# A spectral kernel on one core: halved last inverse step, joined matmul groups, fewer and larger transfers

## The chip, the cores and the metric

The kernel runs on one core of a Trainium2 chip. The core has five engines that work side by side: TensorE (PE, matmuls; its weight loads are listed as PEld), VectorE (DVE), ScalarE (ACT), GpSimd (POOL) and SyncE (SP, which here only issues transfers). Each executes its own instructions strictly in the order of the program and waits on semaphores for the others. Transfers run on 16 DMA engines that the core's queues share. The metric is the time of one execution on the chip in microseconds (us), before and after the change; lower is better.

## The reference

Two independent halves are computed from fp32 inputs and laid side by side in the output (2048 x 1024):

```python
# A: Fourier mixing, 2048 positions x 512 channels
a = jnp.einsum("bsd,ed->bse", x, dft_hid_re)
b = jnp.einsum("bsd,ed->bse", x, dft_hid_im)
y = jnp.einsum("ts,bse->bte", dft_seq_re, a) - jnp.einsum("ts,bse->bte", dft_seq_im, b)
# B: a long convolution of 512 channels over 2048 positions, 128 states per channel
P = jnp.exp((A * dt[:, None])[:, :, None] * pos[None, None, :])
K = 2.0 * jnp.einsum("dn,dnl->dl", C, P).real            # the taps
y = jnp.fft.irfft(jnp.fft.rfft(u_t, L2) * jnp.fft.rfft(K, L2)[None], L2)[:, :, :L]
return y + u * D_skip[None, None, :]
```

## The kernel before

**The stream (class `Fnet`).** Half A is a long run of 1920 matmuls of 128x128 weights on 512 columns, all from line L366. An operand tile is split into a high and a low part (`hi` by ACT at L221, `lo` by DVE at L225), and each product is three matmuls: hi by hi, hi by lo, lo by hi. The stream takes 160 tiles ("items") of 256 KB, 12 matmuls to a tile. Of 160 items 132 come through a buffer `raw` (L334, SP's queue; `RAWS` = 7 of them) and 28 through POOL's queue (`SOFTS`). `DEPTH` = 4 is the number of `hi`/`lo` pairs, so of split tiles waiting for PE. Sums are evacuated by ACT (L389) and stored.

**Half B (class `Ssm`).** DVE builds tables `t1` and `t2` of powers, chunk by chunk, 16 chunks of 32 channels (L605 multiplies, L614 adds, L628, L634). `taps` (L801) multiplies the two tables of a chunk on PE, 128 recorded matmuls on tiles of 128 rows and 32 columns of the array. `stage1_k` (L832) and `stage1_u` (L890) are the first step of the forward transforms of the taps and of the input `u`; they store to DRAM (`xk`, `xu`). The channels are then worked off in four quarters, h = 0 to 3, and each quarter in four parts, q = 0 to 3:

- `load_spectrum` (L965) loads `xt` from `xu` and from `xk`, two transfers of 256 KB each;
- `product` does the second step of the transform (L992, PE), copies to SBUF (L1006, ACT), multiplies the two spectra (L1009, L1011, L1019, L1022, DVE), and does the first inverse step (L1029, PE, on the constant `ia`); ACT copies the sum out (L1044) and `store_z` (L1053) stores `z` to DRAM `zs`, two transfers of 256 KB;
- when all four parts of a quarter are stored, `inverse` runs twice for it: it loads `zl` from `zs`, does the last step (L1078, PE: 16 fp32 matmuls of 128 rows on 64 columns of the array, 128 columns wide, recorded as 32), copies out (L1084) and stores to `out_yb`.

A matmul on plain fp32 operands is recorded twice and each record has its weight load, so L801's 64 matmuls of a chunk are 256 instructions on PE's queue.

**What sets the order.** All engines' programs are written out by one planner (class `Plan`) that runs when the kernel is built. Each piece of work is a generator that yields the engine and the duration it expects; the planner lets the piece that can start first go first, and among those equal to 0.05 us the one of lower urgency number. The stream has urgency 5, so groups of half B are put between its matmuls. `Event` and `Sem` stand for readiness and for buffers. The two double banks of PSUM for half B (`banks`, `give`) are such buffers: a `taps` takes one, a `product` and a first inverse step two each. `Joined` can let a waiting first inverse step ride with the next `taps`: it is then issued directly ahead of it on PE, in the same two banks. With `JOIN` = 0 no quarter does that. `LATE` is the urgency of a quarter's product. The buffers of quarters 0 to 2 (`sets[0]`) exist once; those of `sets[1]` exist twice and are made when the tables' memory is free, after the last taps.

Of the kernel before, what the change touches and what calls it, by code (L numbers as in the profile page):

```python
# [24 lines left out]
def fft_constants():  # L25
# [16 lines left out]
    i = np.zeros((32, 2, 2, 32))  # L42
    i[:, 0, 0], i[:, 0, 1], i[:, 1, 0], i[:, 1, 1] = np.cos(chi), np.sin(chi), -np.sin(chi), np.cos(chi)
    ia = np.tile(i.reshape(32, 2, 64), (4, 1, 1))
    om = 2 * np.pi * ((4 * s[:, None, None] + 1) * (l2[None, :, None] + 32 * l1[None, None, :]) % 8192) / 8192
    ib = np.stack([np.cos(om), -np.sin(om)], axis=1).reshape(128, 32, 64) / 1024
    return [np.ascontiguousarray(a.astype(np.float32)) for a in (f1u, f1k, w2, ia, ib)]
# [3 lines left out]
STREAM = 5  # L51
GRAIN = 0.05
# [3 lines left out]
LATE = 1, 1, 3, 1  # L56
# [26 lines left out]
class Plan:  # L83
# [12 lines left out]
    def step(self, p, value):  # L96
        self.now = p[0]
        while True:
# [15 lines left out]
            else:  # L114
                if r[0] != p[5]:
                    p[0] += HOP
                elif r[0] == "dve" and len(r) < 4:
                    p[0] += RESULT
# [76 lines left out]
class Fnet:  # L195
# [112 lines left out]
    def soft(self, i):  # L308
        return i[0] == "s" and (2 * i[1] + i[2], i[3]) in SOFTS

# [117 lines left out]
class Ssm:  # L428


    def __init__(self, tc, ctx, plan, fnet, nd, ldt, dsk, uG, f1u, f1k, w2, ia, ib, out):
        self.tc, self.nc, self.plan, self.fnet = tc, tc.nc, plan, fnet
        self.nd, self.ldt, self.uG, self.out = nd, ldt, uG, out
# [486 lines left out]
    def quarters(self):  # L920
# [10 lines left out]
        self.plan.spawn(self.products(), 1)  # L931
        for h in range(4):
            self.plan.spawn(self.inverses(h), 1)

    def take(self):
        yield self.xu_ev
        for h in range(3):
            for q in range(4):
                yield self.sets[0].xts
                xt = self.sets[0].pool.tile([128, 2, 4, 2, PART], F32, name="xt")  # L940
                self.xt[h, q] = [[xt[:, r]] for r in range(2)]
                self.plan.set(self.take_ev[h, q])
        for q in range(4):
            self.xt[3, q] = []
            for r in range(2):
                yield self.fnet.x_free[8 + 2 * q + r]
                self.xt[3, q].append(self.fnet.spare(8 + 2 * q + r, [128, 2, 2, PART]))
            self.plan.set(self.take_ev[3, q])

    def spectra(self, name, x, evs):  # L950
        yield self.const2_ev
        yield self.set_ev[0]
        for h in range(4):
            view = x[h].rearrange("(q x g) c l d -> q (g c l) x d", q=8, x=4)
# [26 lines left out]
    def product(self, b, h, q, got, done):  # L981
# [3 lines left out]
        for r in range(2):  # L985
            for c in range(2):
                for xx in range(4):
                    xt = self.xt[h, q][r]
                    xt = (xt[xx * len(xt) // 4])[:, xx % (4 // len(xt))]
# [34 lines left out]
        def run(got):  # L1024
            for c, Y in enumerate((u, t)):
                for g in range(2):
                    for xx in range(4):
                        rows = slice(32 * xx, 32 * xx + 32)
                        nc.tensor.matmul(got[xx // 2][1][64 * g:64 * g + 64, xx % 2, :2 * PART], self.ia[rows, c],  # L1029
# [29 lines left out]
    def inverses(self, h):  # L1059

        yield self.zs_ev[h]
        b = self.sets[h // 3]
# [30 lines left out]
ISSUE = 1.0  # L1093
# [74 lines left out]
```

## Time and profile before

| | |
|---|---|
| median of 3 runs | 582.6 us (582.21 to 583.75) |
| the profiled execution's own time | 582.56 us |
| its span, first to last instruction | 580.8 us |
| granted TensorE clock | 0.999 of full speed |
| PE busy / DVE / ACT / POOL | 571.1 / 512.5 / 371.2 / 40.3 us |
| instructions on PE | 6150 matmul records, 6150 weight loads |
| moved by DMA | 133.10 MB, 229 GB/s mean |

The profile is one execution. Its span is 1.76 us shorter than the time of that execution, which is 0.04 us under the median. Busy shares are means over stages with different limits: the tables fill DVE until about 488 us, and behind them DVE has little to do. A line such as "PE f L1029 x32" in the chain of waits is one group of 32 recorded matmuls; its time there runs from the group's first matmul to the first one of what follows, so it is what the group occupies on PE, while the duration of a single matmul (400 ns in the stream) overlaps with the next.

### The profile page before, as it was taken

To read this page: it belongs to the slowest core of one execution; us is meant where nothing else is said; L and a number is where in the kernel's file an instruction comes from. 1 tells how busy PE (TensorE), PEld (TensorE's weight loads), DVE (VectorE), ACT (ScalarE), POOL (GpSimd) and SP (SyncE) were. 2 spreads that over 40 slices of the span, in tenths; PEclk is the share of its full clock that TensorE was granted. 3 is DMA by queue.
4 is the path that set the end of the run, shared out by engine and by line. 5 is a ranking of instruction groups with operands and counts; after the bars stand their busy time and mean duration, and the time that the engine had idled before them with its cause. 6 is when DMAs were issued, how large, how long until landed. Compare 5 with 4: busy or idle time off the path is not lost.

```text
span 580.8 us, 15376 instructions
## 1 busy us (share of the span) xinstructions
PE 571.1 (98%) x6150; PEld 436.1 (75%) x6150; DVE 512.5 (88%) x911; ACT 371.2 (64%) x729; POOL 40.3 (7%) x60
## 2 busy tenths in 40 slices
PE   8999999999999999999999999999999999999996
PEld 6877777788777777778877777777687777776685
DVE  6999999999999999999999999999989999346410
ACT  4779665763777595768568585945588744445522
POOL 0000000000100000100000001001100000000000
PEclk9999999999999999999999999999999999999999
DMA  8999999986469767876797887479989995789564
GB/s 248 327 372 263 280 294 276 285 262 170 133 159 239 207 171 218 205 180 207 207 222 190 237 216 226 125 186 296 243 280 262 243 282 184 209 251 303 169 195 144
DMA packets 147831, 133.10 MB, mean 229 GB/s; under 512 B 47280, under 2 KB 107312, under 8 KB 147504
## 3 DMA queue, kind: packets, MB, share of 16 engines
q1 hardware_dynamic: 139408, 117.05, 66.7%
q0 software_dynamic: 8064, 14.68, 12.6%
q8 instruction: 48, 0.79, 0.6%
q10 hardware_dynamic: 288, 0.39, 0.2%
q14 instruction: 23, 0.19, 0.1%
HBM read 89.36 MB, written 42.73 MB: 227 GB/s over the span
## 4 chain that ended last, share of the span: by engine, by line
PE 70%; DVE 23%; issue 4%; DMA 2%; SPq 0%; ACT 0%; DVEq 0%; ACTq 0%
PE acc L366 55%; DVE prod L605 8%; DVE t L614 4%; PE f L992 4%; PE f L801 3%; DVE lo L225 3%; PE f L1029 3%; PE f L1078 2%; PE f L890 2%; DVE t L634 1%; PE f L832 1%; DVE z L1009 1%; DVE cs L675 1%; DMA zl<-zs 1%; DVE uk L1011 1%
## 5 line engine op out<-in xcount | busy, mean ns | idle before, releaser
L366 PE MATMUL acc<-hi,x_hi 128*128 128x512 f32 x640 | 258.2, 403 | 0.3 <-ACT hi L221 0.3
L366 PE MATMUL acc<-lo,x_hi 128*128 128x512 f32 x640 | 250.2, 391 | 0.0
L366 PE MATMUL acc<-hi,x_lo 128*128 128x512 f32 x640 | 249.7, 390 | 0.1
L605 DVE TENSOR_TENSOR prod<-t,cs 128x1024 f32<-128x1024 f32 (+4 forms) x192 | 163.1, 867 | 1.7 <-ACT t L723 0.6
L366 PEld LDWEIGHTS acc<-hi,x_hi 128*128 128x128 f32 x640 | 120.1, 188 | 49.8 <-issue 23.7
L366 PEld LDWEIGHTS acc<-hi,x_lo 128*128 128x128 f32 x640 | 120.3, 188 | 26.5 <-DVE x_lo L225 0.5
L366 PEld LDWEIGHTS acc<-lo,x_hi 128*128 128x128 f32 x640 | 120.3, 188 | 23.0 <-DVE lo L225 0.2
L221 ACT ACTIVATE hi<-raw 128x512 fp32r<-128x512 f32 x132 | 82.6, 627 | 64.0 <-PE acc L366 48.5
L225 DVE TENSOR_TENSOR lo<-raw,hi 128x512 fp32r<-128x512 f32 x132 | 90.1, 684 | 28.2 <-ACT hi L221 21.9
L614 DVE TENSOR_TENSOR t<-prod 128x512 f32<-128x512 f32 (+4 forms) x192 | 94.0, 511 | 1.0
L621 ACT ACTIVATE square<-t 128x256 f32<-128x256 f32 (+1 forms) x64 | 36.7, 573 | 31.0 <-DVE t L614 28.3
L320 POOL DMA_DIRECT2D lo<-in_sT x28 | 24.3, 868 | 214.1 <-ACT lo L318 33.8
L1006 ACT ACTIVATE uk<-f 128x1024 f32<-128x1024 f32 x32 | 31.1, 1017 | 11.8 <-PE f L992 11.8
L801 PEld LDWEIGHTS f<-t,t 128*32 128x32 f32 x2048 | 29.5, 110 | 7.9 <-issue 5.8
L801 PE MATMUL f<-t,t 128*32 128x64 f32 x2048 | 32.4, 220 | 1.9 <-issue 1.4
L389 ACT ACTIVATE y<-acc 128x512 f32<-128x512 f32 x47 | 28.0, 595 | 8.7 <-PE acc L366 8.6
L1009 DVE TENSOR_TENSOR z<-uk 128x512 f32<-128x512 f32 x32 | 21.9, 684 | 9.6 <-ACT uk L1006 7.4
L315 POOL DMA_DIRECT2D hi<-in_sT x28 | 16.2, 577 | 189.4 <-PE acc L366 147.0
L1044 ACT ACTIVATE z<-f 128x512 f32<-128x512 f32 x32 | 17.7, 592 | 13.3 <-PE f L1029 13.3
L634 DVE TENSOR_TENSOR t<-square 128x128 f32<-128x128 f32 (+1 forms) x64 | 24.6, 385 | 0.0
L992 PE MATMUL f<-xt,w 64*32 64x256 f32 x768 | 23.5, 379 | 0.0
L1011 DVE TENSOR_TENSOR uk<-uk 128x512 f32<-128x512 f32 x32 | 22.1, 690 | 0.9
(94 smaller groups left out, 490.7 us busy)
## 6 DMA issues: line engine op xcount, KB each, us to landing
raw<-in_sT SPq DMA_DIRECT2D x99, 256.0 KB, 5.4
p<-y SPq DMA_DIRECT2D x32, 256.0 KB, 3.2
xk<-xk_sb SPq DMA_DIRECT2D x32, 256.0 KB, 5.2
zs<-z SPq DMA_DIRECT2D x32, 256.0 KB, 3.3
zl<-zs SPq DMA_DIRECT2D x16, 512.0 KB, 5.0
raw<-p SPq DMA_DIRECT2D x32, 256.0 KB, 4.4
hi<-in_sT POOLq DMA_DIRECT2D x28, 256.0 KB, 4.6
lo<-in_sT POOLq DMA_DIRECT2D x28, 256.0 KB, 4.9
```

The costliest lines, as they stand in the source:

```text
L221: self.nc.scalar.activation(hi, src, AF.Copy)
L225: self.nc.vector.tensor_tensor(lo, src, hi.bitcast(F32), op=OP.subtract)
L366: nc.tensor.matmul(acc[d], l[:, cols], r, start=k == 0 and n == 0, stop=k == len(items) - 1 and n == 2)
L389: self.nc.scalar.activation(y, ps, AF.Copy, scale=-1.0 if g[2] == 1 else 1.0)
L605: self.nc.vector.tensor_tensor(p.rearrange("p k d c m -> p k (d c) m"), src.rearrange("p d c l -> p (d c) l")[:, None, :, rows].to_broadca ...
L614: self.nc.vector.tensor_tensor(dst[:, :, :, rows], p[:, 0], p[:, 1, :, ::-1], op=OP.add)
L621: self.nc.scalar.activation(sq, t[:, :, :, m // 2:m], AF.Square)
L634: self.nc.vector.tensor_tensor(t[:, :, 0, m:2 * m:2], box[0][:, :, 0], box[0][:, :, 1], op=OP.subtract)
L801: nc.tensor.matmul(ps[32 * j:32 * j + 32, i], t1[:, d, c], t2[:, d, c], start=c == 0, stop=c == 1, tile_position=(0, 32 * j))
L992: nc.tensor.matmul(got[r][1][32 * xx:32 * xx + 32, g, 256 * c:256 * c + 256], self.w2[rows, 2 * q + r, xx, 32 * c:32 * c + 32], xt[rows].r ...
L1006: a.activation(uk[:, r].rearrange("p g c n d -> p g (c n d)"), p, AF.Copy)
L1011: v.tensor_tensor(t[:, r], t[:, r], u[:, r, :, ::-1], op=OP.mult)
```

## The change

What it does, part by part:

1. **The last inverse step of quarters 2 and 3 is halved.** The 64 rows of z are taken as two halves: every second output position needs only their sum and the others only their difference. `inverse2` loads `zl` with the two halves side by side, DVE forms their sum (`zsum`) and difference (L1095, L1097 of the new kernel, four instructions of 128x512 to an inverse), and PE multiplies them with a new constant `ib2`, on tiles of 64 rows and 32 columns of the array: 32 fp32 matmuls of 128 columns, recorded as 64, in place of 16 recorded as 32. The constant `ia` gets a second half that carries the phase this needs. `ib2` (512 KB) is loaded when the tables' memory is free. Both quarters use the doubled buffers of `sets[1]`.
2. **The first inverse step of quarters 0 and 1 rides with taps** (`JOIN` from 0 to 2): eight groups of 32 records go directly ahead of eight `taps`.
3. **Spectra and z in half as many transfers:** 512 KB in one instead of 256 KB in two, for `xt` of quarters 0 to 2 and for all `zs`.
4. **Numbers of the planner:** `RAWS` from 7 to 5, `DEPTH` from 4 to 5, the urgency of quarter 2's product from 3 to 1. The set `SOFTS` holds the same 28 items as before. The planner writes the whole program anew.

Line numbers in what follows are the new kernel's where the row is marked as such: L366 becomes L370, L801 L805, L992 L998, L1029 L1035, L1053 L1058, L965 L970, L225 L229, L1022 L1028; the last step of quarters 0 and 1 is L1126 and that of 2 and 3 L1104.

In PE's order a joined group has no stream between its two halves. Before, the first group of the first inverse step in the program (its last rows here; `f` are the two double banks, `uk` the product) was followed by the stream (L366):

```order
L1029 MATMUL f_2429<-uk,ia 64x256 x2
L1029 MATMUL f_2430<-uk,ia 64x256 x2
L366 MATMUL acc<-hi,x_hi_322 128x512
L366 MATMUL acc<-lo,x_hi_322 128x512
L366 MATMUL acc<-hi,x_lo_323 128x512
```

After, the same group (now L1035) is followed at once by the 64 matmuls of a taps (L805, on the two tables `t`), and then the stream (L370):

```order
L1035 MATMUL f_2575<-uk,ia 64x256 x2
L1035 MATMUL f_2576<-uk,ia 64x256 x2
L805 MATMUL f_2575<-t_124,t_2083 32x64 x64
L370 MATMUL acc<-hi,x_hi_452 128x512
L370 MATMUL acc<-lo,x_hi_452 128x512
```

The first inverse step has moved to the front of a taps. Over the whole program the stretches of stream between such groups fall from 72 to 63.

At the end of PE's order, before, the very last step of the last quarter was 16 matmuls on `zl`:

```order
L366 MATMUL acc<-hi,x_lo_5734 128x512
L1078 MATMUL f_7331<-zl,ib 64x128 x16
L366 MATMUL acc<-hi,x_hi_5770 128x512
L366 MATMUL acc<-lo,x_hi_5770 128x512
L366 MATMUL acc<-hi,x_lo_5771 128x512
```

After, it is 32 matmuls of half the rows and half the columns of the array, in pairs that take the sum and the difference by turns (the last two pairs here):

```order
L1104 MATMUL f_7402<-zsum,ib_6661 32x128 x2
L1104 MATMUL f_7402<-zl,ib_6661 32x128 x2
L370 MATMUL acc<-hi,x_hi_5551 128x512
L370 MATMUL acc<-lo,x_hi_5551 128x512
L370 MATMUL acc<-hi,x_lo_5552 128x512
```

Behind the last such group stand 15 stream matmuls before and 9 after; between the last group of the first inverse step and the first last-step group behind it stand 66 before and 78 after.

On DVE the new rows (`zsum`, `zl`) stand in the last part of the program, the first eight between the products of quarter 3 (one stretch of it after the change):

```order
L1097 TENSOR_TENSOR zl<-zl 128x512
L1015 TENSOR_TENSOR z<-uk 128x512
L1017 TENSOR_TENSOR uk<-uk 128x4x128
L1095 TENSOR_TENSOR zsum<-zl 128x512
L1097 TENSOR_TENSOR zl<-zl 128x512
```

All sixteen stand behind the last row of the tables. Up to and with that row DVE's program has 855 instructions before and 854 after, and they differ by kind in one row: 136 splits of the stream (L225) before, 135 after.

The diff, cut to its core:

```diff
-LATE = 1, 1, 3, 1
+LATE = 1, 1, 1, 1
...
     def load_spectrum(self, name, h, q, view):
         yield "dma", load(512, 270), FAST
-        for r in range(2):
-            for p, xt in enumerate(self.xt[h, q][r]):
-                n = xt.shape[1]
-                self.nc.sync.dma_start(xt[:, :, "uk".index(name)], view[2 * q + r, :, n * p:n * p + n])
+        for p, xt in enumerate(self.xt[h, q]):
+            n = xt.shape[1]
+            self.nc.sync.dma_start(xt[:, :, "uk".index(name)], view[q, :, n * p:n * p + n])
         self.plan.set(self.xt_ev[name, h, q])
...
-                        nc.tensor.matmul(got[xx // 2][1][64 * g:64 * g + 64, xx % 2, :2 * PART], self.ia[rows, c],
+                        nc.tensor.matmul(got[xx // 2][1][64 * g:64 * g + 64, xx % 2, :2 * PART], self.ia[rows, q // 2 if h >= HALVED else 0, c],
                                          Y[rows, :, g, 0], start=c == 0, stop=c == 1, tile_position=(32 * xx, 64 * g))
...
     def store_z(self, h, q, t, sem):
-        view = self.zs[h].rearrange("(q x g) c l d -> q (g c l) x d", q=8, x=4)
+        view = self.zs[h].rearrange("(q x g) c l d -> q (g c l) x d", q=4, x=8)
         yield "dma", load(512, 270), FAST
-        for r in range(2):
-            self.nc.sync.dma_start(view[2 * q + r], t[:, r])
+        self.nc.sync.dma_start(view[q], t.rearrange("p r x d -> p (r x) d"))
...
         yield self.zs_ev[h]
-        b = self.sets[h // 3]
+        if h >= HALVED:
+            yield self.ib2_ev
+        b = self.sets[int(h >= min(HALVED, 3))]
         for i in range(2):
             yield b.zls
-            self.plan.spawn(self.inverse(b, h, i, 16), 1)
+            self.plan.spawn((self.inverse2 if h >= HALVED else self.inverse)(b, h, i, 16), 1)
+
+    def load_ib2(self):
+        yield self.set_ev[1]
+        yield self.zs_ev[1]
+        self.ib2 = self.sets[1].pool.tile([128, 16, 2, 32], F32, name="ib2")
+        yield "dma", load(512)
+        self.nc.sync.dma_start(self.ib2, self.ib2_in)
+        self.plan.set(self.ib2_ev)
+
+    def inverse2(self, b, h, i, n):
+
+        nc, c = self.nc, n // 2
+        z = b.pool.tile([128, 2, c, PART], F32, name="zl", bufs=b.n)
+        view = self.zs[h].rearrange("(a s) c l d -> (s c) a l d", a=2)
+        yield "dma", load(64 * n, 270), FAST
+        for y in range(2):
+            o = n * i + c * y
+            nc.sync.dma_start(z[64 * y:64 * y + 64], view[:, :, o:o + c])
+        t = b.pool.tile([128, c, PART], F32, name="zsum", bufs=b.n)
+        for w in range(0, c, 4):
+            m = slice(w, w + 4)
+            yield "dve", dve(512)
+            nc.vector.tensor_tensor(t[:, m], z[:, 0, m], z[:, 1, m], op=OP.add)
+            yield "dve", dve(512), *APART
+            nc.vector.tensor_tensor(z[:, 1, m], z[:, 0, m], z[:, 1, m], op=OP.subtract)
+        (k, ps), = yield from self.banks(1)
+        yield "pe", 1.06, None, 64
+        for o in range(0, c, 2):
+            for x in range(4):
+                for y in range(2):
+                    r, w = slice(64 * y, 64 * y + 64), o + x // 2
+                    nc.tensor.matmul(ps[32 * x:32 * x + 32, y, PART * (o // 2):PART * (o // 2) + PART],
+                                     self.ib2[r, c * i + w, x % 2], (t, z[:, 1])[x % 2][r, w], start=True, stop=True,
+                                     tile_position=(64 * y, 32 * x))
+        for y in range(2):
+            yield "act", act(512)
+            nc.scalar.activation(z[:, 0, 4 * y:4 * y + 4].rearrange("p w d -> p (w d)"), ps[:, y], AF.Copy)
+        self.give(k)
+        yield "dma", load(32 * n, 270)
+        nc.sync.dma_start(self.out[:, c * i:c * i + c, PART * h:PART * h + PART], z[:, 0])
+        self.plan.put(b.zls)
...
-CHUNK, FIRST, JOIN = 32, 128, 0
-RAWS, DEPTH, STAGED, AHEAD = 7, 4, 4, 3
+CHUNK, FIRST, JOIN = 32, 128, 2
+HALVED = 2
+RAWS, DEPTH, STAGED, AHEAD = 5, 5, 4, 3
```

More of the change, by code (lines that the diff above doesn't have):

```diff
@@ L939, in take @@
                 yield self.sets[0].xts
-                xt = self.sets[0].pool.tile([128, 2, 4, 2, PART], F32, name="xt")
-                self.xt[h, q] = [[xt[:, r]] for r in range(2)]
+                xt = self.sets[0].pool.tile([128, 8, 2, PART], F32, name="xt")
+                self.xt[h, q] = [xt]
                 self.plan.set(self.take_ev[h, q])
@@ L1126, in layout @@
     n = lambda a: np.asarray(a)
-    f1u, f1k, w2, ia, ib = fft_constants()
+    f1u, f1k, w2, ia, ib, ib2 = fft_constants()
     w = np.stack([n(A_dft_hid_re).T, n(A_dft_hid_im).T])
```

45 lines of the change are left out of this document (27 added, 18 removed).

## The prediction

> **What bounds the kernel now.** I read the page's busy times and slices first, then busy time by window, then the chain of waits, and at last single stretches of the timeline.
>
> ```profile
> span 580.8 us, 15376 instructions
> PE 571.1 (98%) x6150; PEld 436.1 (75%) x6150; DVE 512.5 (88%) x911; ACT 371.2 (64%) x729; POOL 40.3 (7%) x60
> ...
> DVE  6999999999999999999999999999989999346410
> ...
> 0.00:488.00 488.00, 483.20 (x5178) 370.22 (x5179) 476.46 (x855) 333.83 (x669) 40.27 (x60) 1.00 0.82 234
> 488.00:581.00 93.00, 87.92 (x974) 65.88 (x972) 36.00 (x57) 37.41 (x60) 0.00 (x0) 0.99 0.68 206
> ```
>
> The window rows give length, then PE, PEld, DVE, ACT, POOL, then the granted clock. Two engines are full until 488 us: PE idles 4.8 us of 488, DVE 11.5. Behind that DVE is busy 36.0 us of 93 and PE goes on alone at full clock. The border is the last row of the tables and the last taps:
>
> ```profile
> 487.48 0.68 DVE L614 TENSOR_TENSOR t<-prod 128x512 f32<-128x512 f32 x1
> ...
> 488.41 1.99 PE L801 MATMUL f<-t,t 128*32 128x64 f32 x128
> ```
>
> DVE ends its last table row at 488.16, a quarter of a microsecond before PE takes it up. So the time is the start of the last taps, which both engines set within that quarter, plus what PE still has to do, plus a tail. From the chain of waits (start, what the group occupies, count):
>
> ```profile
> 488.48 1.92 PE f L801 x128
> 490.40 2.26 PE acc L366 x9
> 492.67 1.05 PE f L1029 x32
> ...
> 497.03 11.79 PE acc L366 x51
> 508.82 1.90 PE f L1078 x32
> ...
> 516.38 1.89 PE f L992 x64
> ...
> 572.29 3.64 PE acc L366 x15
> ```
>
> A stream matmul costs (11.79 - 2.26) / (51 - 9) = 0.227 us, and a stretch of stream costs 2.26 - 9 x 0.227 = 0.22 us on top: the price of leaving and re-entering the stream. PE ends at 572.29 + 3.64 = 575.93, 87.45 us after the start of the last taps; the tail to the end of the span is 4.87 us.
>
> **The change part by part. Halved last step.** Four groups of 64 records take the place of four of 32 that occupy 1.90 us each. The nearest row is L992, the same tiles of 64 rows and 32 columns of the array: 64 records on 256 columns in 1.89. At 128 columns half its streaming remains: with 0.2 of entry and drain, 1.69 / 2 + 0.2 = 1.05 us. L1029, with half the records at the same 256 columns, agrees: 1.05. Gain 4 x 0.85 = 3.4 us. The bounds: nothing, if a record costs what it costs in L992 whatever its width; and 4 x (1.90 - 64 x 1.92 / 128) = 3.8 us at L801's pace of 15 ns to a record. I take 3.4, by L992's tile shape.
>
> [...]
>
> **Its DVE rows.** Sixteen rows of 128x512:
>
> ```profile
> L1009 DVE TENSOR_TENSOR z<-uk 128x512 f32<-128x512 f32 x32 | 21.9, 684 | 9.6 <-ACT uk L1006 7.4
> ```
>
> 16 x 0.684 = 10.9 us, all behind the last table row, where DVE idles 57 us. What they can delay is the last chain of quarter 3, from its z to the end:
>
> ```profile
> 551.80 1.09 ACT L1044 ACTIVATE z<-f 128x512 f32<-128x512 f32 x2 [2.18 <-PE f L1029]
> ...
> 556.20 1.76 SPq L1073 DMA_DIRECT2D zl<-zs  x4
> ...
> 566.85 1.97 PE L1078 MATMUL f<-zl,ib 128*64 128x128 f32 x32
> ...
> zs<-z SPq DMA_DIRECT2D x32, 256.0 KB, 3.3
> zl<-zs SPq DMA_DIRECT2D x16, 512.0 KB, 5.0
> ```
>
> After: copies 1.1, z's transfer at most 5.0 (512 KB, as `zl`), two issues 0.9 (four take 1.76), `zl` 5.0, four DVE rows 2.7: 14.7 us, against 78 stream matmuls, 17.9 us. Hidden with 3 us to spare; if the store's and load's landings grew by more than that, the excess would land on the end. The second half is wanted 3 us later and DVE gives it 2.7 later.
>
> **Joined groups and order.** Nine stretches of stream fewer, 9 x 0.22 = 2.0 us; one of them lies behind the last taps, eight ahead. The change of tiles between L1029 and L801 is never seen directly here, so the bounds are 0 and 9 x 0.3. More matters ahead of the taps: the first inverse step no longer starts as soon as its product is nearly ready. Before it did, and waited in the middle:
>
> ```profile
> 0.00:581.00 581.00, 20.24 (x512) 10.08 (x512) 1.00 0.80 229
> ...
> 547.29 1.12 PE L1029 MATMUL f<-uk,ia 32*64 32x256 f32 x32
> ...
> PE f L801 <- issue: 1.4, 1, 1.4
> PE f L832 <- DVE ks L824: 0.6, 1, 0.6
> ```
>
> The first row is PE's and PEld's busy time on line L1029 alone: 20.24 us for 16 groups, where an undisturbed one takes 1.12: 2.3 us of waiting on DVE. By the new order DVE has finished the product several rows ahead of each joined group, so I take the 2.3 us as gone, and the 0.6 at L832, whose rows also stand farther apart; bounds 0 and 2.9.
>
> **Instruction supply.** The 1.4 us of "issue" is one taps that ran dry:
>
> ```profile
> 405.56 1.88 PE L801 MATMUL f<-t,t 128*32 128x64 f32 x118
> 408.86 0.41 PE L801 MATMUL f<-t,t 128*32 128x64 f32 x10 [1.43 <-issue]
> ...
> q8 instruction: 48, 0.79, 0.6%
> ```
>
> 48 instruction transfers for 12300 instructions on PE is one to 256. A taps alone is 256 instructions in 1.92 us; joined it is 320 in 2.97, without the slow stream to catch up in. One of 16 taps ran dry before; of the eight long ones and the others I take three, 4.3 us in place of 1.4, two ahead of the last taps and one at it. Bounds: none, and all eight.
>
> [...]
>
> **Transfers, buffers, ranks.** Half the transfers for `xt` and `zs` move the same bytes; SP saves some 40 issues, and no group on PE waits long for a transfer, so I cost them at nothing. What covers a spectrum is the stream ahead of its product; if that cover went, one landing 1.7 us later (5.0 against 3.3) would be the price each time, for at most 12. `raw` falls by two and `hi`/`lo` rises by one pair, which brings splits nearer to PE's need earlier; nothing. `ib2` is 512 KB ahead of one `raw` on SP; nothing, at most one landing of 5.0 us, which five pairs in stock, 12 matmuls or 2.7 us each, cover. Quarter 2's earlier product doesn't delay the tables: 854 DVE rows stand up to the last table row, where 855 did.
>
> **The sum.** Start of the last taps: by PE, 488.48 + 12 more stream matmuls ahead of it (2.7) - 8 stretches (1.8) - 2.9 of waits on DVE - 1.4 of the old dry run + 2.9 of two new ones = 488.0. By DVE, one split fewer, 488.5 - 0.7 = 487.8. The later sets it: 488.0. Behind it: 87.45 - 12 stream matmuls (2.7) - 3.4 - one stretch (0.2) + one dry run (1.4) = 82.5. Tail 4.9: the last 512 KB of output leaves nearer to the end, but the last transfer is still the stream's. Span 575.4. The profiled execution took 582.56 for a span of 580.8, 1.76 more, and stands 0.04 under the median of 582.6: forecast 577.2 us, 0.9% faster.
>
> **Rivals.** (1) *The halved step isn't halved*: a record costs 29.5 ns as in L992 and the four groups stay at 1.89. For it: same tiles. Against: L801's 15 ns. Time 577.2 + 3.4 = 580.6, chance 0.04. A floor between the two paces, say 22 ns, leaves part: 64 x 0.022 + 0.2 = 1.6 us, 577.2 + 4 x 0.55 = 579.4, chance 0.03. [...]
>
> (2) *Banks.* A joined group holds both double banks until ACT has made three copies, and the next product needs both.
>
> ```profile
> L221 ACT ACTIVATE hi<-raw 128x512 fp32r<-128x512 f32 x132 | 82.6, 627 | 64.0 <-PE acc L366 48.5
> ```
>
> Three copies (two of L1044 take 1.09) are 1.6 us, two splits between them 1.25: 2.9, where the shortest stretch of stream behind a joined group is 12 matmuls, 2.7. With a hop on either side say 0.4 us for each of eight: 3.2, 580.4. Against: an item needs one split in 2.7 us, so mostly one stands between. Chance 0.09.
>
> (3) *Slower: instruction supply.* All eight joined groups run dry: five more than in the forecast, 577.2 + 5 x 1.43 = 584.4. With seven (582.9) the old time is back; the eighth makes it slower. For it: 320 instructions in a row exceed a transfer of 256. Against: the next transfer may already be there. Chance 0.08.
> (4) *The gain is eaten ahead of the taps* by waits that the planner didn't see, with the last taps 6 us later: 583. Chance 0.04.
>
> **Chances and range.** The forecast's case has 0.72; its own range is 573 (no dry run: DVE's 487.8 + 81.1 + 4.9 + 1.8 = 575.6, less 2.5 if DVE's 11.5 us of idle time shrink by a fifth) to 579.5. A difference of 0.3%, 1.75 us, is about what a measurement of this kernel can tell from none. Faster than that (under 580.85): the forecast, most of (1) and (2), 0.86; within it 0.06; slower 0.08. The range, 573.0 to 581.0, leaves out (3), (4) and the far ends of the others.
>
> **What would show it.** Right: groups of L1104 at 1.05 us, the last taps near 488, 82 us from there to PE's last matmul, PE's time on L1035 at 1.1 us to a group. Wrong: L1104 near 1.9; "issue" on L805 in more than four places; PE's waits on ACT copies ahead of L998; the last taps past 492.

## The result, and the profile after

The changed kernel takes 585.39 us (median of 9 runs, 583.77 to 589.58), the kernel before 582.40 on the same chip (9 runs, 581.67 to 584.42). The ratio is 1.0054, 95% interval 1.0036 to 1.0072: about half a per cent slower, where 577.2 us and 0.9% faster were forecast. The profiled execution of the changed kernel took 584.71 us, its span is 582.9.

The page of the changed kernel, busy times and two of its slices:

```profile
span 582.9 us, 15613 instructions
PE 567.2 (97%) x6278; PEld 434.4 (75%) x6278; DVE 524.8 (90%) x927; ACT 371.5 (64%) x729; POOL 40.5 (7%) x60
...
DVE  6999999999999999999999898999998999747723
...
PEclk9999999999999999999999899999999999999999
```

PE is busy for 3.9 us less than before, as the change meant, and yet the span is 2.1 us longer: PE waits more. New are the 8s in DVE's row, which was full up to the last table row, and one 8 in the granted clock, in the 23rd of the 40 slices (from 320.6 us). From the chain of waits of the changed kernel (start, us, what):

```profile
494.64 1.97 PE f L805 x128
...
537.76 9.12 DMA zs<-z
...
547.63 2.29 PE f L1104 x123
...
571.15 1.09 PE f L1104 x64
...
574.52 1.08 PE f L1104 x64
575.60 1.69 PE acc L370 x7
```

The last taps start at 494.6 us; before it was 488.5, forecast were 488.0. PE ends at 577.9 (the chain leaves the last two matmuls out), 83.3 us later; before 87.45, forecast 82.5. The halved groups take 1.09 us each against 1.90. So the stretch behind the last taps shrank nearly as forecast, and the start of the last taps slipped by 6.2 us. Where it slipped, PE's waits tell (the engine, the tile and line that waited, the releaser: us in total, times, longest):

```profile
PE f L1035 <- ACT zl L1132: 3.0, 1, 3.0
PE f L998 <- DMA raw<-in_wT: 1.8, 1, 1.8
...
PE f L1104 <- ACT z L1050: 1.3, 1, 1.3
PE acc L370 <- DMA lo<-in_sT: 1.2, 2, 0.8
PE acc L370 <- ACT y L393: 0.8, 1, 0.8
PE f L836 <- DVE ks L828: 0.4, 1, 0.4
PE f L805 <- issue: 0.4, 1, 0.4
```

The second row is the wait of a product (L998) at 416 us; its releaser is put down to another load of that moment, but what the product lacked was its spectrum, as the experiments show. The largest wait stands at 320 us. PE's timeline there (start, us, instructions, the wait before them and its releaser):

```profile
319.43 0.65 PE L1035 MATMUL f<-uk,ia 32*64 32x256 f32 x4
323.08 1.11 PE L1035 MATMUL f<-uk,ia 32*64 32x256 f32 x28 [3.00 <-ACT zl L1132]
324.12 3.57 PE L805 MATMUL f<-t,t 128*32 128x64 f32 x128
```

Busy time of the changed kernel by window, cut where the clock changes (length, PE, PEld, DVE, ACT, POOL, then the granted clock, third number from the right):

```profile
320.64:324.05 3.41, 0.97 (x28) 0.58 (x28) 3.41 (x6) 2.91 (x7) 1.28 (x2) 1.00 0.59 82
324.06:327.46 3.40, 3.40 (x134) 3.34 (x128) 3.37 (x5) 0.96 (x2) 0.00 (x0) 0.50 1.04 277
327.47:330.88 3.41, 3.41 (x38) 2.44 (x38) 1.84 (x4) 3.12 (x9) 0.00 (x0) 1.00 0.38 108
```

A joined group starts in the one free double bank, then waits 3.00 us for ACT to empty the other, in which the last step L1126 of quarter 0 lies. And the taps behind it take 3.57 us in place of 1.92, with no wait: the granted clock is 0.50 in that window and 1.00 on either side. So this place costs 3.6 us at the group, 3.0 of them the wait, and another 1.6 at the taps. The stretch at 0.50 lasts 3.41 us, and in the 3.41 us ahead of it PE is busy for 0.97.

ACT's rows of the same place show why the copy was late:

```profile
315.29 0.50 ACT L662 ACTIVATE seed<-seed 128x352 f32<-128x352 f32 x1 [2.94 <-DVE seed L660]
315.81 1.28 ACT L664 ACT_TABLE_LOAD   x1
317.10 0.50 ACT L664 ACTIVATE seed<-seed 128x352 f32<-128x352 f32 x1
317.62 1.28 ACT L666 ACT_TABLE_LOAD   x1
...
321.44 0.57 ACT L1132 ACTIVATE zl<-f 128x512 f32<-128x512 f32 x1
```

ACT waited 2.94 us for DVE's row L660 of a seed, then went through the seed's functions with two table loads (1.28 us each) and three rows of other work among them (0.6 us each), and only then came to the copy, whose bank PE had filled by 317.2.

### The profile page after: what moved, and what is told of

Its sections match the earlier page's. It is cut to its first block, busy times and chain, and to the rows that moved or that the text cites. A ratio compares the mean times of both kernels' runs of the same rounds, so it can differ in the third digit from the quotient of the medians.

```text
span 582.9 us, 15613 instructions
## 1 busy us (share of the span) xinstructions
PE 567.2 (97%) x6278; PEld 434.4 (75%) x6278; DVE 524.8 (90%) x927; ACT 371.5 (64%) x729; POOL 40.5 (7%) x60
## 4 chain that ended last, share of the span: by engine, by line
PE 57%; DVE 29%; issue 5%; DMA 4%; ACT 4%; DVEq 0%; ACTq 0%
PE acc L370 45%; DVE prod L609 10%; DVE t L618 6%; DVE lo L229 4%; PE f L998 3%; PE f L805 3%; PE f L1035 2%; PE f L894 2%; DMA zs<-z 2%; DVE t L638 1%; DVE z L1015 1%; DVE t L632 1%; PE f L1126 1%; DVE xk_sb L848 1%; DMA raw<-in_wT 1%
## 5 line engine op out<-in xcount | busy, mean ns | idle before, releaser
L370 PE MATMUL acc<-hi,x_hi 128*128 128x512 f32 x640 | 257.5, 402 | 0.9 <-ACT y L393 0.8
L370 PE MATMUL acc<-lo,x_hi 128*128 128x512 f32 x640 | 250.4, 391 | 1.2 <-DMA lo<-in_sT 1.2
L370 PE MATMUL acc<-hi,x_lo 128*128 128x512 f32 x640 | 249.9, 390 | 0.0
L609 DVE TENSOR_TENSOR prod<-t,cs 128x1024 f32<-128x1024 f32 (+3 forms) x192 | 163.5, 869 | 5.1 <-ACT t L747 3.1
L370 PEld LDWEIGHTS acc<-hi,x_hi 128*128 128x128 f32 x640 | 120.2, 188 | 47.9 <-issue 20.5
L370 PEld LDWEIGHTS acc<-hi,x_lo 128*128 128x128 f32 x640 | 120.3, 188 | 26.8 <-issue 0.4
L370 PEld LDWEIGHTS acc<-lo,x_hi 128*128 128x128 f32 x640 | 120.4, 188 | 25.2 <-DMA lo<-in_sT 2.1
L225 ACT ACTIVATE hi<-raw 128x512 fp32r<-128x512 f32 x132 | 81.6, 626 | 58.6 <-PE acc L370 45.1
L229 DVE TENSOR_TENSOR lo<-raw,hi 128x512 fp32r<-128x512 f32 x132 | 90.0, 684 | 23.2 <-ACT hi L225 18.6
L805 PEld LDWEIGHTS f<-t,t 128*32 128x32 f32 x2048 | 31.0, 114 | 6.7 <-issue 2.3
L805 PE MATMUL f<-t,t 128*32 128x64 f32 x2048 | 33.9, 226 | 0.4 <-issue 0.4
L998 PE MATMUL f<-xt,w 64*32 64x256 f32 x768 | 23.5, 379 | 1.8 <-DMA raw<-in_wT 1.8
L632 DVE SCALAR_TENSOR_TENSOR t<-t 128x128 f32<-128x128 f32 (+2 forms) x48 | 22.3, 466 | 0.5
```

Source lines behind the costliest of these rows:

```text
L225: self.nc.scalar.activation(hi, src, AF.Copy)
L229: self.nc.vector.tensor_tensor(lo, src, hi.bitcast(F32), op=OP.subtract)
L370: nc.tensor.matmul(acc[d], l[:, cols], r, start=k == 0 and n == 0, stop=k == len(items) - 1 and n == 2)
L609: self.nc.vector.tensor_tensor(p.rearrange("p k d c m -> p k (d c) m"), src.rearrange("p d c l -> p (d c) l")[:, None, :, rows].to_broadca ...
L632: self.nc.vector.scalar_tensor_tensor(t[:, :, 1, m:2 * m:2], t[:, :, 0, m // 2:m], 2.0, t[:, :, 1, m // 2:m], op0=OP.mult, op1=OP.mult)
L805: nc.tensor.matmul(ps[32 * j:32 * j + 32, i], t1[:, d, c], t2[:, d, c], start=c == 0, stop=c == 1, tile_position=(0, 32 * j))
```

## An account of PE's losses

To compare orders with each other, each kernel's PE time is taken apart in the same way: a stream matmul counts 0.2275 us, leaving and re-entering the stream 0.2, an undisturbed group 1.92 (taps), 1.05 (first inverse step), 1.90 (last step), 1.09 (halved) and 1.89 (product). What a group or stretch occupies beyond that is its loss (waits, "issue" and low clock alike). The groups of the first transform step (L836 and L894 of the new kernel) are left out; they lose 1.7 us before and 1.9 after. The kernel before loses 7.3 us in the profiled execution, the changed one 14.3. The work itself shrank by 4 x 0.81 = 3.2 us for the halved step and by about 2.0 for nine stretches. 580.8 - 5.2 + 7.0 = 582.6, and the tail is 0.2 longer: the span of 582.9 is accounted for. The losses of the changed kernel, place by place: 3.6 and 1.6 at the joined group and its taps at 319 to 328 us, 1.9 at the spectrum at 412, 1.4 at the first halved group at 545, 3.1 between 136 and 181 (before: 1.3 there), 0.6 at a taps at 354, and the rest under 0.6 each but for 1.2 at the start, which both have. Gone are the waits of the first inverse step on DVE (2.7) and the taps at 405 us with 1.43 us of "issue" in it (1.7).

| kernel | median us | ratio to before, 95% | last taps, us | PE's losses, us |
|---|---|---|---|---|
| before | 582.4 to 582.9 | 1 | 488.4 | 7.3 |
| changed | 585.4 | 1.0054 [1.0036, 1.0072] | 494.6 | 14.3 |
| e2 no halving | 587.9 | 1.0081 [1.0068, 1.0094] | 494.9 | 13.7 |
| e3 two transfers | 583.6 | 1.0016 [1.0002, 1.0030] | 493.9 | 12.0 |
| e4 halving alone | 581.0 | 0.9964 [0.9951, 0.9976] | 488.3 | 8.7 |
| e5 sines moved | 584.4 | 1.0020 [1.0001, 1.0040] | 492.6 | 12.7 |
| e6 joining alone | 600.7 | 1.0302 [1.0279, 1.0325] | 485.9 | 26.8 |
| e7 = e3 and e5 | 582.4 | 1.0013 [0.9985, 1.0041] | 491.9 | 12.1 |
| e8 halving, one transfer | 580.4 | 0.9959 [0.9945, 0.9972] | 488.3 | 8.1 |
| e9 = e7, t2's rows first | 581.7 | 0.9996 [0.9974, 1.0019] | 490.4 | 11.6 |
| e10 = e8, buffers 5 and 5 | 608.7 | 1.0442 [1.0421, 1.0462] | 482.2 | 31.1 |
| e11 = e8, planned anew | 585.9 | 1.0063 [1.0040, 1.0085] | 492.4 | 14.6 |
| e12 = e9, t1's row first | 581.7 | 0.9990 [0.9974, 1.0006] | 491.7 | 11.7 |
| e13 = e8, buffers for z | 580.9 | 0.9969 [0.9957, 0.9982] | 487.7 | 7.9 |

The median of before is that of the chip that ran the row's kernel. The ratio goes with the means of the runs, not with the medians: e7's runs average 583.4 us and before's on that chip 582.7. The last taps and losses are of one profiled execution each, and those of e3, e5 and e10 were 1.6, 1.3 and 5.7 us faster than their medians; in e6, e10 and e11 other work stands ahead of the last taps, so that only time and losses compare.

## The experiments

The theories at the start: A, the joined groups need both double banks, so ACT's copies in ACT's order, and this delays taps and tables; B, the larger transfers land later; C, any newly planned order comes out worse; D, the halved step's own rows and constant cost time.

**e2: no halving.** Quarters 2 and 3 use the plain last step.

```diff
-HALVED = 2
+HALVED = 4
```

> The changed kernel with the halved step off (HALVED = 4), so that quarters 2 and 3 use the plain last step again; joined groups, transfers and the planner's numbers as changed, and the order up to the last taps the same. Theory A (the joined groups, which need both double banks and so ACT's copies in order, delay the tables): the last taps stay at 494 to 495 us, and the time grows by the halving alone, 4 x (1.90 - 1.09) = 3.2 us, less the wait of 1.4 us at the first halved group if that goes with it: 586.5 to 588.6 us. Rival D (the halved step's own constant, buffers and DVE rows delay the tables): the last taps come back to 488 or 489 us and the time is 582 to 584 us.

587.88 us, as A had it. The last taps stay, at 494.86 us, and so do the waits for the banks and at the spectrum of 416 us (PE's waits in e2):

```profile
PE f L1035 <- ACT zl L1132: 2.7, 1, 2.7
PE f L998 <- DMA raw<-in_wT: 1.8, 1, 1.8
```

The halved step has no part in the slip (D falls), and it is worth 2.5 us of time in this order (587.88 - 585.39; the two ran on different chips, and by the ratios to before it is 1.6), 2.8 of span: the 3.2, less 0.6 that PE loses more with it.

**e3: two transfers** of 256 KB for each spectrum and each z, in the changed kernel's order.

```diff
-            self.nc.sync.dma_start(xt[:, :, "uk".index(name)], view[q, :, n * p:n * p + n])
+            for m in range(0, xt.shape[1], n):
+                o = xt.shape[1] * p + m
+                self.nc.sync.dma_start(xt[:, m:m + n, "uk".index(name)], view[q, :, o:o + n])
...
-        self.nc.sync.dma_start(view[q], t.rearrange("p r x d -> p (r x) d"))
+        for r in range(2):
+            self.nc.sync.dma_start(view[q, :, 4 * r:4 * r + 4], t[:, r])
```

> The changed kernel with two transfers of 256 KB again for each spectrum and each z; same plan on PE, DVE and ACT. Theory A: the last taps stay at 494 us within half a microsecond; of PE's wait of 1.9 us for a spectrum at L998 and of 1.4 us at L1104 a part goes, so the time is 583 to 585.5 us. Rival B (the larger transfers, which land later, delay the products and with them the tables): the last taps at 488 to 490 us, the time 577 to 581 us.

583.55 us, inside A's interval; B as the cause of the slip falls, since the last taps come at 493.9. Of the two waits on transfers one shrank and one went, and the joined group still waits (PE's waits in e3):

```profile
PE f L1037 <- ACT zl L1135: 3.2, 1, 3.2
...
PE f L1000 <- DMA xt<-xk: 0.7, 1, 0.7
```

**e4: halving alone**, with no joined groups, two transfers, and `RAWS`, `DEPTH` and `LATE` of before. PE's order up to the last taps is that of the kernel before.

```diff
-LATE = 1, 1, 1, 1
+LATE = 1, 1, 3, 1
...
-CHUNK, FIRST, JOIN = 32, 128, 2
+CHUNK, FIRST, JOIN = 32, 128, 0
...
-RAWS, DEPTH, STAGED, AHEAD = 5, 5, 4, 3
+RAWS, DEPTH, STAGED, AHEAD = 7, 4, 4, 3
```

> The halved step alone: no joined groups, two transfers, RAWS 7, DEPTH 4 and the urgencies of the kernel before. Theory A: the last taps are at 488.5 us within 0.7, and the stretch behind them is 87.45 less 4 x 0.81 = 84.2 us, so the time is 582.4 - 3.2 = 579.2 us, with 578.0 to 580.5 as bounds. Rival C (any newly planned order comes out some microseconds worse, whatever is changed): last taps past 491 us, time 582 to 585 us. Rival D (the halved step's rows and constant cost time): likewise 582 us and more, but with the loss behind the last taps.

580.96 us, a little over A's upper bound: 0.36% faster than before, not 0.55%. The last taps start at 488.34 as expected, so what is missing lies behind them. PE loses about 1 us at the first two halved groups, 0.6 of it in waits for ACT and DVE; their place in the chain of waits of e4 is this:

```profile
527.80 9.62 DMA zl<-zs
...
537.44 0.70 DVE zsum L1098
...
545.43 0.66 PE f L1107 x28
```

The load of `zl` ends 9.6 us after the step before it in the chain, and then eight rows of the halved step stand between DVE's other rows for 8 us. These rows were costed as hidden; at the last halved group they are, at the first one not quite. The tail is 0.9 us longer too.

**e5: three sine instructions moved.** In the changed kernel ACT's L666 (with its table load), L668 and L670 of one seed go behind the two copies L1132 for which the joined group waited; nothing else changes its place on any engine.

```diff
-        a.activation(r[:, 0:6], r[:, 0:6], AF.Sin, scale=-TWO_PI)
+        self.later(ck, lambda: a.activation(r[:, 0:6], r[:, 0:6], AF.Sin, scale=-TWO_PI))
...
-        self.give(k)
+        self.give(k), self.flush()
...
+    def later(self, ck, op):
+        if ck == 11:
+            self.held.append(op)
+        else:
+            op()
```

> The changed kernel with one thing moved: ACT's three sine instructions of one seed (L666 with its table load, L668, L670) stand behind the two copies L1132 for which the joined group at 319 us waited 3.0 us. Every other instruction keeps its place on its engine. Theory A: the joined group there waits 0.7 to 1.3 us instead of 3.0, DVE's gaps of 0.88 and 0.71 us behind it shrink, the last taps come at 492 to 493.2 us and the time is 583.0 to 584.0 us, 1.4 to 2.4 less than the changed kernel. Rival (the wait at 319 us is caught up or covered by another engine before the last taps, so it costs nothing): last taps at 494 to 495 us, the time as the changed kernel's within 0.6 us.

584.4 us, the last taps at 492.58: 2.0 us earlier, inside A's interval, though the median is 1.0 less than the changed kernel's rather than 1.4 to 2.4 (by the ratios to before on each one's chip, 2.0). The wait and the low clock are gone together. The joined group in e5's timeline:

```profile
320.99 1.11 PE L1035 MATMUL f<-uk,ia 32*64 32x256 f32 x28 [0.27 <-ACT zl L1132]
```

And e5's windows:

```profile
320.00:324.00 4.00, 3.37 (x133) 2.22 (x136) 3.93 (x8) 3.81 (x7) 0.86 (x1) 1.00 0.82 115
324.00:328.00 4.00, 4.00 (x80) 3.01 (x76) 3.96 (x6) 3.13 (x8) 0.00 (x0) 1.00 0.76 217
```

So at this place the low clock came with the wait. But of the 5.2 us that the place cost, only 2.0 reach the last taps; the group and its taps still lose 1.5, and 1.2 more are lost at the spectrum of 412 us, which the product now reaches earlier than its load lands (PE's waits in e5):

```profile
PE f L998 <- DMA raw<-in_wT: 3.0, 1, 3.0
```

**e7: both edits together.**

> The changed kernel with both single edits together: two transfers of 256 KB for each spectrum and each z, and ACT's three sine instructions behind the copies that the joined group at 319 us waits for. If the two waits are separate and add up: no clock below 0.95 ahead of 500 us, last taps at 491 to 492.3 us, the stretch behind them 81 to 82 us, time 579.5 to 582 us. If a wait that is taken away only moves to another place (a PE wait of over 2 us elsewhere): last taps past 493 us and 583 us or more.

582.35 us (the first reading had an upper bound of 582), the last taps at 491.85, no clock under 0.95 ahead of 500 us. On the last taps the two edits add up: 0.6 us in e3 alone, 2.0 in e5 alone, 2.7 of the 6.2 us together. But the second reading came true in part: PE's wait for the spectrum is 2.1 us, as the next experiment shows, longer than e3's 0.7, because the product now comes to it earlier. The stretch behind the last taps is 83.8 us, not 81 to 82, with 1.0 us of waiting at the first halved group again.

**e9 and e12: the rows of the next tables first.** DVE's largest gap in the joined order is 1.6 us at 358 us, ahead of the first rows of the next tables. e9 lets ACT write t2's first rows ahead of its copies for z and ks there, e12 the row of t1 too (the last line of the diff is e12's).

```diff
+            (h, q, n) == (1, 1, 0) and self.first_rows(11); a.activation(z[:, :, 2 * n:2 * n + 2].rearrange("p r x d -> p x r d"),
...
+    def first_rows(self, n):
+        a, cs, t = self.nc.scalar, self.cs[n], self.t2
+        a.activation(t[:, :, :, 1].rearrange("p d c -> p c d"), cs[:, :, 0, :, 0], AF.Copy)
...
+        self.early = self.tab.tile([128, CHUNK, 2, 32], F32, name="t1", bufs=2)
```

> The kernel with both single edits, and one more thing moved: at 356 us ACT writes the first rows of the next table t2 (L747, L750) ahead of the two copies of z (L1052), the copy of the taps (L815) and the seed's L684, not behind them; nothing else changes its place. Theory A (in the joined order ACT's copies for half B stand ahead of the rows for which DVE waits): DVE's gap of 1.62 us there goes or falls below 0.5, the last table row and the last taps come 1.0 to 1.6 us earlier, at 490.3 to 490.9 us, and the time falls by about as much, to 580.8 to 581.5 us. Rival (another engine sets the last taps, DVE's gap is spare time): last taps at 491.5 us or later, the time as with both edits alone (582.35) within 0.6 us.

> As the kernel before it in this series, but the one copy L727 (first row of the next t1, which DVE's second row there reads) goes ahead of the copies of z and of the taps as well. In that kernel DVE's gap at 357.7 us stayed at 1.76 us, now put down to L727. Theory A: the gap falls below 0.5 us and the last table row comes 1.0 to 1.6 us earlier than the 490.35 us there, if the load of a spectrum at 409 us lands alike (PE's wait there 0.7 us): last taps 488.9 to 489.5, time 580.2 to 580.9 us. Rival (the gap is spare time, and the 1.4 us by which the last taps came earlier there were the load's alone): last taps at 490 us or later, the time 581.65 within 0.6 us.

In e9 the last taps came at 490.42 us, as A had it, but not for A's reason: the gap stayed, and the time of 581.65 us lies between the two readings. In e12 it stayed too, and the last taps were back at 491.65, with 581.74 us, as the rival had it. DVE's row behind the gap, which waited 1.62 us for ACT's L747 in e7, in e9's timeline:

```profile
359.49 0.40 DVE L609 TENSOR_TENSOR prod<-t,cs 128x128 f32<-128x128 f32 x1 [1.76 <-ACT t L727]
```

And in e12's:

```profile
359.65 0.38 DVE L609 TENSOR_TENSOR prod<-t,cs 128x128 f32<-128x128 f32 x1 [1.72 <-ACT cs L684]
```

What holds DVE there is `cs`, whose second half ACT's L684 writes when DVE's L679 has written the first. In e12 L679 is done at 357.6 us, and L684 starts at 358.7, behind the very copies of z and ks (ACT's rows in e12):

```profile
357.21 1.06 ACT L1052 ACTIVATE z<-f 128x512 f32<-128x512 f32 x2
358.18 0.58 ACT L815 ACTIVATE ks<-f 128x512 f32<-128x512 f32 x1
358.66 0.96 ACT L684 ACTIVATE cs<-cs 128x352 f32<-128x352 f32 x2
```

The two edits moved other rows and left L684 where it was. So they don't test this part of A; by these rows about 1.0 of the 1.72 us is still the copies' (an estimate). What did move the last taps was the load of a spectrum. PE's wait for it in e7:

```profile
PE f L1000 <- DMA xt<-xk: 2.1, 1, 2.1
```

In e9:

```profile
PE f L1000 <- DMA xt<-xk: 0.7, 1, 0.7
```

And in e12:

```profile
PE f L1000 <- DMA xt<-xk: 1.6, 1, 1.6
```

Waits of 2.1, 0.7 and 1.6 us, last taps at 491.85, 490.42 and 491.65: between e7 and e9 the wait goes over to the last taps one to one, between e7 and e12 for less than half, and it differs by 1.4 us between three executions whose orders differ by a few copies on ACT. In these orders the product of quarter 2 follows its load closely: the load is issued at about 407 us, and PE is at the product at 413. In the changed kernel it is issued at 409.4, behind the landing of the store of `xk` from which it reads, and lands at 417.6. In the kernel before the load of this product is issued at 404.4 and lands at 411.8, and the product comes at 416.8: the landing takes 7 to 8 us in both, but there the stream covers it.

**e8: halving alone, one transfer each.** e4 with the single transfers of 512 KB.

> The halved step alone (no joined groups, RAWS 7, DEPTH 4, the urgencies of before), but with spectra and z in one transfer of 512 KB each, as in the changed kernel. If the larger transfers cost time by themselves: about 1.8 us more than the halved step alone with two transfers (581.0), so 582 to 584 us, with waits of PE for xt at L998 or for z behind the last taps. If they only cost where a product follows close on its load, as in the joined order: 580.4 to 581.6 us, no difference that can be told.

580.39 us, no difference from e4's 580.96 that can be told: in this order the larger transfers cost nothing that the times show. Its median is the lowest of all, 0.41% below before (0.28 to 0.55%); e4 and e13 can't be told from it.

**e13: buffers for z.** In e8 ACT's copy at 543 us waits until the store of the z before it has landed, and PE with it (e8's chain of waits):

```profile
534.42 8.89 DMA zs<-z
...
543.42 0.61 ACT z L1050
```

```diff
-        z = b.pool.tile([128, 2, 4, PART], F32, name="z", bufs=b.n)
+        z = self.sets[1].pool.tile([128, 2, 4, PART], F32, name="z2", bufs=2) if h == 2 and 1 in self.sets else b.pool.tile([128, 2, 4, PART], F32, name="z", bufs=b.n)
```

> The halved step alone with one transfer each, and two further buffers for z of quarter 2 (from the memory of the tables, once they are done), so that ACT's copy L1050 at 543 us needn't wait until the store of the z before it has landed (8.9 us in the chain of waits). The order is the same on every engine. If that wait is what the single store costs: PE's wait of 1.2 us ahead of the first halved group goes, and the time falls from 580.4 to 579.2 us, with 578.7 to 579.9 as bounds. If another wait takes its place: 580.4 within 0.4 us.

580.9 us, no gain, and 0.1 above the second reading's bounds: another wait took its place. PE's waits at the first halved groups are 0.7 us in sum where they were 1.1, what it loses there is 1.1 where it was 1.2, and the chain runs as in e4, over the load of `zl` (10.19 us in it) and the halved step's rows on DVE. PE's waits in e13:

```profile
PE f L1104 <- ACT z L1050: 0.4, 1, 0.4
PE f L1104 <- DVE zl L1097: 0.3, 1, 0.3
```

**e6: joining alone.** The kernel before with `JOIN` 2 in place of 0.

> The kernel before with one number changed, JOIN from 0 to 2: the eight first inverse steps of quarters 0 and 1 ride with taps, nothing else is edited, and the planner writes the order anew (60 stretches of stream in place of 72, two products fewer ahead of the last taps, so the start of the last taps isn't comparable with the other kernels and PE's waits are read instead). If the joined groups are worth what the forecast took, the 12 stretches and the waits on DVE that go make it 2.6 to 5 us faster: 577.5 to 580 us. Theory A: one or more waits of PE for ACT at the first rows of a joined group (L1029) of over 1 us, PE's waits ahead of the last taps longer in sum than before by 3 us or more, and a time of 582 to 587 us.

600.7 us, far outside both readings. The waits of A aren't what costs it: the longest on ACT at a joined group is 0.7 us, and PE's losses ahead of the last taps are 10.6 us, 3.3 more than before. The time is lost at the end, where this order has no stream left to cover a last step (e6's chain of waits):

```profile
577.72 1.14 PE f L1029 x28
...
580.41 2.85 DMA zs<-z
...
583.32 3.95 DMA zl<-zs
...
587.41 6.61 PE f L1078 x64
```

**e10 and e11: planned anew.** Both are e8, so without joined groups, with one thing changed: the buffers (5 and 5), or 0.01 us of one cost of the planner.

```diff
-RAWS, DEPTH, STAGED, AHEAD = 7, 4, 4, 3
+RAWS, DEPTH, STAGED, AHEAD = 5, 5, 4, 3
```

```diff
-HOP, RESULT, LATENCY = 0.3, 0.15, 3.3
+HOP, RESULT, LATENCY = 0.31, 0.15, 3.3
```

> The halved step alone with one transfer each and no joined groups, but RAWS 5 and DEPTH 5 as in the changed kernel (7 and 4 in the kernel before). The program up to 190 us holds no joined group in any of the kernels, so PE's losses between 130 and 170 us are read: the changed kernel lost 3.1 us there, the halved step alone 2.0 us. If the buffers' numbers are the cause: about 3 us here too, with waits for lo. If not: about 2 us. For the whole time, by the buffers' theory 582 us or more, by theory A 580 to 582 us; the planner writes another order behind 200 us, so the time decides less than the stretch.

> The halved step alone with one transfer each, and one cost of the planner changed by 0.01 us (HOP from 0.30 to 0.31), which does nothing but make it write another order. Theory A: without joined groups another order stays within about 1.5 us of the 580.4 us of that kernel, and PE waits nowhere for ACT over 2 us. Rival C (any new order loses some microseconds against one that was searched for, so that the change's loss says nothing of the joined groups): 583 us or more, with several waits of over 1 us at new places.

e11 takes 585.85 us, 5.5 more than e8, as C had it: the number itself does nothing but write another order. Of C's several waits of over 1 us there is one, of 3.0, with a low clock behind it (an 8 in the 29th of the 40 slices), and one of 1.0, at places of their own (PE's waits in e11):

```profile
PE f L998 <- DMA xt<-xk: 3.6, 2, 3.0
...
PE f L1104 <- DVE zsum L1095: 1.0, 1, 1.0
```

e10 takes 608.7 us; besides waits for `hi` and `lo` (3.9 and 4.0 us) it ends, like e6, with last steps that no stream covers. Between 130 and 170 us it loses 2.7 us, the changed kernel 3.1, e8 2.0: that doesn't tell the buffers' part apart. One wait of 0.8 us there (L370 for ACT's y) stands in all kernels with 5 and 5, and in none of the others.

What follows of all this. The slip of the last taps is made of single waits that were found: the largest, the banks at 319 us with the low clock behind them, was mostly taken away; the one for the spectrum at 412 was shortened, but lasts the longer the earlier PE comes to it. The two edits brought 2.7 us back, and 4.2 in e9, where the load landed early. That joined groups as such cost time is not shown: seven of the eight don't wait for a bank, and their saving of nine stretches is there. C is what the runs support best: the four orders that the planner wrote anew (the changed kernel's with its five edited forms, e6, e10 and e11) lost 11.6 to 31 us on PE, with joined groups or without, and e4, e8 and e13, which kept the order of before up to the last taps, lost 7.9 to 8.7. Only e11 is a new order and nothing else, so C rests on one clean case. A change of `LATE` alone was not run. Left open is how much of the loss a joined order must have; with the two edits it still starts its last taps 2.1 to 3.5 us later than e8.

## Why the prediction was wrong

- **What bounds the kernel** was read rightly: the start of the last taps, what PE still has to do, and a tail. The step that failed is the first term of the sum, *start of the last taps 488.0*; it was 494.6. In the sum's own terms, the 12 stream matmuls and the eight stretches are as counted, and the waits of the first inverse step on DVE are mostly gone: the line of PE on L1035 has 18.55 us where L1029 had 20.24. What the sum lacked are new waits: without its two dry runs it comes to 485.1, and PE came to the last taps 9.5 us after that. The sum had 2.9 us for two dry runs and nothing else. What stands there are 5.2 us at the banks at 319 us with the low clock, 1.9 at a spectrum, 1.8 more than before between 136 and 181 us, with waits of PE for `lo` and for ACT's y whose cause stays open, and 0.6 at a taps.
- **Halved last step**: right. 3.4 us were forecast, 3.2 measured, 17 ns from one record to the next. Rival 1 falls, and with it its floor of 22 ns, which was an estimate: 64 records take 1.09 us, where the floor had 1.6.
- **Its DVE rows**, "hidden with 3 us to spare": at the last chain of quarter 3 yes, PE comes to it without a wait. The chain that wasn't worked out, quarter 2's, has 1.3 us of waiting. The transfer was mis-sized: z's store was taken at 5.0 at most and holds its buffer for 9.1 us in the chain.
- **Joined groups and order**: 63 stretches, as counted. That a joined group holds both banks was put among the rivals at 0.4 us for each of eight. In place of that, seven show no wait for a bank and one 3.0 us, for a reason that the rival didn't have: ACT's order, with a seed ahead of the copy, not the number of copies.
- **Instruction supply**: wrong. Three dry taps of 1.43 us were forecast; the trace has 0.4 us of "issue". That the 1.43 us of "issue" before were a lack of instructions was the author's estimate, from 48 transfers for 12300 instructions; no run shows their cause. The one long taps that looks like a dry run (3.57 us) stands in the window with a clock of 0.50. Rival 3 falls with it.
- **Transfers at nothing**: wrong by the 1.8 us at the spectrum, close to the 1.7 that the prediction named as the price of one lost cover. That `LATE`, which lets quarter 2's product come early, gave the cover up is likely, but was not tested by itself. e8 shows no cost of the size in the order of before (580.39 us against e4's 580.96).
- **Behind the last taps**: 83.3 against 82.5, errors that nearly cancel: no dry run there (1.4 less), but 1.4 at the first halved group, 0.5 at L836 and 0.2 of the halving.
- **Rivals and chances**: what came is rival 4, the gain eaten ahead of the taps with the last taps 6 us later, at a chance of 0.04. It was held so small because the planner's order was taken at its word; the kernel before was the only order whose losses had been seen.

## What to carry to other kernels

Where a planner writes the whole program anew, the new order is the largest part of the change, and the waits of the old order say little of the new one's: price it by how much other orders lose, or change one part while the order stays, as the halved step alone did here for 0.4%. When a bank or buffer is freed by an engine with work in order, look at what stands ahead of the freeing instruction on that engine, not only at how long the copy takes. And a wait on TensorE can come with a cost beyond its length: behind waits of 3.0, 2.7 and 3.2 us in three traces here the taps took 1.6, 1.3 and 1.6 us longer at half the clock, behind one of 2.99 us in e5 the clock stayed at 1.00.

## What the hardware showed

- Waits of PE of 3.0, 2.7 and 3.2 us at 320 us (changed kernel, e2, e3) each came with a stretch at half the clock, and the taps in it took 1.6, 1.3 and 1.6 us longer. A wait of 2.99 us at 413 us in e5 was followed by a clock of 1.00.
- In the changed kernel the trace's record of the clock has only the values 1.00 and 0.50: 1.00 up to 324.06 us, 0.50 for the 3.41 us to 327.47, then 1.00 up to 580.06, which is behind PE's last matmul. In e3 three windows of 4 us from 320 us on have 0.67, 0.50 and 0.98, which makes 6.8 us at 0.50 if its clock has the same two values (an estimate). In the changed kernel PE is idle for 2.4 of the 3.41 us ahead of the low clock. In e5 the wait of 2.99 us lies across two windows of 3.41 us, and PE is idle for 1.4 and 1.5 us of them (e5's windows):

```profile
411.17:414.58 3.41, 1.97 (x9) 1.30 (x7) 3.38 (x5) 2.13 (x7) 0.55 (x1) 1.00 1.12 323
414.59:418.00 3.41, 1.87 (x64) 1.34 (x64) 2.91 (x6) 0.03 (x1) 0.00 (x0) 1.00 1.05 341
```

The clock is 1.00 in both. Why it fell at the one wait and not at the other is not shown.

- In the orders written anew the runs of one kernel scatter: nine of the changed kernel from 583.77 us at a mean clock of 0.998 to 589.58 at 0.990, e11's twelve, without a joined group, from 582.14 at 0.998 to 589.31 at 0.991, where e4's five lie between 580.42 and 581.67 at 0.997 to 0.999. Of each kernel one execution was traced, so what lowered the clock in the longer runs is not shown.
- In the changed kernel the halved groups (L1104), on tiles of 64 rows and 32 columns, have 64 records of 128 columns in 1.09 us, 17 ns apart; the product's (L998), on the same tiles, 64 of 256 columns in 1.89 us, 29.5 ns apart.
